# Linear attention and a GEGLU block on one core: block 1's halved units parted at column 320, one attention tile moved ahead of a transposing load, preps spread, one input load moved to another queue

## The chip, the cores and the metric

The kernel runs on one core of one Trainium2 chip. A core has TensorE (PE in the profile, its weight loads as PEld), VectorE (DVE), ScalarE (ACT), GpSimd (POOL) and SyncE (SP, which here only issues DMAs), and 16 DMA engines that all queues share. The metric is the device time of one execution in microseconds. Times are medians over several executions. A difference under about 0.3%, here 1 us, is about what a measurement of this kernel can't tell from no change.

## The reference

There are 8 batches of 8 heads, 576 positions, 64 features. The attention has no softmax; it is a product with cosine weights:

```python
theta = pi/2 * pos / S
phi(x) = concat([relu(x) * cos(theta), relu(x) * sin(theta)], axis=-1)   # 64 -> 128 features
kv  = einsum('bhsf,bhsd->bhfd', phi(k), v);   z = sum(phi(k), axis=2)
out = einsum('bhsf,bhfd->bhsd', phi(q), kv) / (einsum('bhsf,bhf->bhs', phi(q), z) + 1e-6)
```

The output, reshaped to 4608 tokens of 512, goes through a GEGLU block with 1536 hidden features: `(gelu(x @ w_gate) * (x @ w_val)) @ w_out`. Inputs and output are float32.

## The kernel before, in words

Everything on TensorE is in bf16. The 4608 tokens are cut into 9 blocks of 512 tokens, while a batch has 576, so blocks and batches drift apart by 64 tokens a batch: block 1 holds the last 64 tokens of batch 0 and the first 448 of batch 1, and block 2 holds the last 128 tokens of batch 1 and the first 384 of batch 2.

For a batch b these steps come in order:

- `prep` (lines 152 to 164) makes phi(q) and phi(k): for each of 9 position groups j, one instruction on VectorE for the cosine half (line 162) and one on ScalarE for the sine half (line 160), 128 x 256 each. This text writes them as q(b) and k(b) preps.
- `turn_q(b)` (line 191) turns phi(q) with two DMA transposes issued by SP (line 193) into `qT`. There is one `qT` buffer, so the next batch's transposes must wait until TensorE has read the last of the batch before.
- `kv_unit(b)` (line 235): 72 small matmuls (line 241) sum phi(k) and v, with a column of ones for z.
- `nm_unit(b, t)` (line 280), for each of five tiles t of 128 rows: 8 matmuls (line 282) for numerator and denominator, then on VectorE the added epsilon, the reciprocal and the product (lines 293 to 295) that gives the tile x(b, t).
- `turn_x(b, t)` (line 346) turns x(b, t) with DMA transposes by SP (line 349) into the columns of `xT` of one or two blocks; each block has its own `xT` buffer, three in turn.

For a block n, twelve units `gv_unit(n, jt)` (line 391) make the hidden features: 4 matmuls with gate weights into one PSUM bank, 4 with value weights into another (line 400), gelu on ScalarE (line 408, into `gel`) and the product on VectorE (line 409, into `hT`). Two pairs of banks alternate, so a unit's gate matmuls wait for the gelu of the unit two before it, and its value matmuls for that unit's product. `o_part` (line 427) does the output product (line 430), one third of a row tile between two units, and `store` (line 415) writes it out by SP.

All instructions stand in program order on each engine, and the order is written out by hand in the main loop (line 607 on). In the first blocks the first units are halved by columns (`heads`, line 616), since the later columns of `xT` come late: block 1 has six units halved at column 256 (`HALF`), run as six first halves and then six second halves. Columns 0 to 319 of block 1 need x(0,4), x(1,0) and x(1,1), which TensorE turns; columns 320 to 511 need x(1,2) and x(1,3), which the DMA transposes of line 349 bring. In the same stretch VectorE and ScalarE do the q(2) and k(2) preps, VectorE casts v(2) (line 179), and TensorE does the last tile of batch 1, `nm_unit(1, 4)`, after the sixth half. Its transposes `turn_x(1, 4)` are issued two steps later, followed by output stores.

The inputs come by two kinds of queue. GpSimd issues the weights and batches 1 and 2 and q(3) early on (lines 459 to 478); each input of a batch is loaded in two halves of 576 KB. SP issues batch 0, k(3), v(3), and then q, k and v of each later batch right after the turn of the batch before (`loads`, line 590, called in line 682). The staging buffers are two for each of q, k and v. The load of q(4) therefore goes into the buffer of q(2).

Of the kernel before, what the change touches and what calls it, by code (L numbers as in the profile page):

```python
# [16 lines left out]
def kernel(  # L17
# [13 lines left out]
    nc = tc.nc  # L31
# [8 lines left out]
    R = S // 64  # L40
    NB = B * S // 512
    NT = 5
    EPS = 1e-6
    BLK = 512
# [26 lines left out]
    def rows(t, b):  # L71
        return t[b].rearrange("(m i) (p j) d -> (i p) m (j d)", i=2, j=R)
# [4 lines left out]
    def load(eng, name, b, m0, m1, j0=0, j1=R):  # L77
        if (name, b) not in staged:
            staged[name, b] = inp.tile([128, NP, R * D], FP32, name=name + "f")
        eng.dma_start(  # L80
            out=staged[name, b][:, m0:m1, j0 * D:j1 * D],
            in_=rows(srcs[name], b)[:, m0:m1, j0 * D:j1 * D],
        )
# [51 lines left out]
    gate = consts.tile([128, 1], FP32)  # L135
# [16 lines left out]
    def prep(name, b, part, js, m0=0, m1=NP, eng=None):  # L152
        dst = phi_tile(name, b)
        src = staged[name, b]
        tab = (cos_t, sin_t)[part]
        for j in js:
            o = dst[:, m0:m1, j, part * D:(part + 1) * D]
            i = src[:, m0:m1, j * D:(j + 1) * D]
            if eng is nc.scalar:
                nc.scalar.activation(o, i, AF.Relu, scale=tab[:, j:j + 1])  # L160
            else:
                (eng or nc.vector).tensor_scalar(  # L162
                    o, i, 0.0, tab[:, j:j + 1], op0=ALU.max, op1=ALU.mult
                )
# [26 lines left out]
    def turn_q(b):  # L191
        for i in range(2):
            nc.sync.dma_start_transpose(
                out=qt_tile(b)[:, i].rearrange("f m (j p) -> f (m j) p", p=64),
                in_=phi["q", b][64 * i:64 * i + 64].rearrange("p m j f -> p (m j f)"),
            )
# [83 lines left out]
    def nm_unit(b, t, b0=6):  # L280
        for h in range(H):
            nc.tensor.matmul(  # L282
                bank(b0 + h // 4)[:, (h % 4) * (D + 1):(h % 4 + 1) * (D + 1)],
                lhsT=q_cols(b, t, h),
                rhs=kv_sb[b][:, h // 2, h % 2, :],
                start=True,
                stop=True,
            )
        nm = ps[:, b0:b0 + 2, 0:4 * (D + 1)].rearrange("p g (h d) -> p g h d", h=4)
        den = attn2.tile([128, 2, 4], FP32, name="den")  # L290
        rec = attn2.tile([128, 2, 4], FP32, name="rec")
        x = xsp.tile([128, 2, 4, D], BF16, name="x_sb")
        nc.vector.tensor_scalar_add(den, nm[:, :, :, D], EPS)
        nc.vector.reciprocal(rec, den)  # L294
        nc.vector.tensor_tensor(  # L295
            x,
            nm[:, :, :, 0:D],
            rec[:, :, :, None].to_broadcast([128, 2, 4, D]),
            op=ALU.mult,
        )  # L300
        xs[b, t] = x.rearrange("p g h d -> p (g h d)")
# [30 lines left out]
    def xT_block(blk):  # L332
        if blk not in xT:
            xT[blk] = xtp.tile([128, CT, BLK], BF16, name="xT")
        return xT[blk]
# [55 lines left out]
    def gv_unit(n, jt, c0=0, w=BLK):  # L391
        xt = xT[n]
        js = slice(jt * 128, (jt + 1) * 128)
        b0 = 2 * (turn[0] % 2)
        turn[0] += 1
        if n not in hT:
            hT[n] = ffn.tile([128, JT, BLK], BF16, name="hT")
        for g, wt in ((0, wg_sb), (1, wv_sb)):
            for ct in range(CT):
                nc.tensor.matmul(  # L400
                    bank(b0 + g)[:, 0:w],
                    lhsT=wt[:, ct, js],
                    rhs=xt[:, ct, c0:c0 + w],
                    start=(ct == 0),
                    stop=(ct == CT - 1),
                )
        gel = ffn.tile([128, BLK], FP32, name="gel")
        nc.scalar.activation(gel[:, 0:w], bank(b0)[:, 0:w], AF.Gelu)  # L408
        nc.vector.tensor_mul(  # L409
            hT[n][:, jt, c0:c0 + w], gel[:, 0:w], bank(b0 + 1)[:, 0:w]  # L410
        )
# [10 lines left out]
    def flush(n=4):  # L422
        for i, o_sb in stores[:n]:
            store((nc.sync, nc.sync), i, o_sb)
        del stores[:n]
# [19 lines left out]
    HALF = BLK // 2  # L445
# [144 lines left out]
    def loads(b, names=("q", "k", "v")):  # L590
        for name in names:
            for m in (0, 2):
                load(nc.sync, name, b, m, m + 2)
# [13 lines left out]
    for n in range(1, NB):  # L607
        b = n + 1
        t_kv, t_nm, t_q, t_k = {1: (7, 9, 12, 12), 2: (6, 7, 7, 9), 3: (2, 5, 6, 9)}.get(
            n, (1, 2, 4, 8)  # L610
        )
        for jt in range(JT):
            if n == 1 and jt >= t_nm:
                nm_unit(2, jt - t_nm, (6, 4, 6)[jt - t_nm])
                turn_x(2, jt - t_nm)
            heads = (0, 6, 4, 2)[n] if n < 4 else 0
            if jt >= heads:
                gv_unit(n, jt)
            else:
                for i in range(2):  # L620
                    half, unit = divmod(2 * jt + i, heads)
                    gv_unit(n, unit, half * HALF, HALF)
                    if n == 1 and jt < 2:
                        js = ((4,), (5,), (6,), (7, 8))[2 * jt + i]
                        prep("q", b, 1, js, eng=nc.scalar)
                        prep("q", b, 0, js)
                    if n == 1 and jt > 1:
                        j = 2 * jt - 4 + i
                        prep("k", b, 0, (j,))
                        prep("k", b, 1, (j,), eng=nc.scalar)  # L630
            if jt % 3 == 1 and n > 1:
                flush()
            if b < B:
                if n == 1 and jt == 1:
                    turn_q(b)
                if n == 1 and jt == 2:
                    nm_unit(1, NT - 1)
                if n == 1 and jt == 3:
                    turn_x(1, NT - 1)
                    flush()  # L640
                nms = [(b, jt - t_nm)] if n > 1 and 0 <= jt - t_nm < NT else []
                if n == 2 and jt < 2:
                    nms.append((n, 3 + jt))

                late = -(-(BLK - 64 * b) // 128)
                i = jt - t_nm - 1
                if n > 1 and 0 <= i < late:
                    turn_x(b, i)
                if n == 1 and jt == JT - 1:
                    loads(3, ("k", "v"))  # L650
                for bt in nms:
                    nm_unit(*bt)
                if jt == t_kv:
                    kv_unit(b)
                if n == 1 and jt == 6:
                    prep("k", b, 0, (R - 1,))
                    prep("k", b, 1, (R - 1,), eng=nc.scalar)
                if n == 2 and 3 <= jt < 6:
                    prep_third("k", b, jt - 3)
                i = 2 * (jt - 5) if n == 1 else jt - (4 if n == 2 else 0)  # L660
                if n == 1 and i == 0:
                    cast_v(b, 0, 4, dve_copy)
                if n in (2, 3) and 0 <= i < 2:
                    cast_v(b, 2 * i, 2 * i + 2, dve_copy)
                i = jt - 9
                if n > 2 and 0 <= i < 2 and b + 1 < B:
                    cast_v(b + 1, 2 * i, 2 * i + 2, dve_copy)
                if (n, jt) in q3:
                    cosines, sines_ = q3[n, jt]
                    prep("q", 3, 1, sines_, eng=nc.scalar)  # L670
                    prep("q", 3, 0, cosines)
                if n > 1 and b + 1 < B:
                    if 0 <= jt - t_q < 3:
                        prep_third("q", b + 1, jt - t_q)
                    if 0 <= jt - t_k < 3:
                        prep_third("k", b + 1, jt - t_k)
                for c, t in nms:
                    if t == NT - 1:
                        if c + 1 < B:
                            turn_q(c + 1)  # L680
                        if c + 2 < B:
                            loads(c + 2)
                        for i in range(-(-(BLK - 64 * c) // 128), NT):
                            turn_x(c, i)
            if n > 1:
                o_part(
                    4 * (n - 1) + jt // 3,
                    range(4 * (jt % 3), 4 * (jt % 3) + 4),
                    4,
                    act_copy,  # L690
                )
# [47 lines left out]
```

## Time and profile before

| what | value |
|---|---|
| median of 6 executions | 326.8 us (325.78 to 327.68) |
| the profiled execution | 325.78 us, of which the span is 323.6 us |
| granted TensorE clock | 0.999 |
| PE busy | 316.8 us (98% of the span) |
| DVE, ACT, POOL busy | 171.0, 159.0, 27.4 us (53%, 49%, 8%) |
| DMA | 53.83 MB, mean 166 GB/s |
| block 1's halved units | about 54.5 to 65.3 us after the span's start |
| block 1's full units, with kv_unit(2) | 65.3 to 77.9 us |
| first halved unit of block 2 | 77.85 us |

In the lines of the profile, "L400 PE MATMUL ps<-xT,wg_sb" means line 400, engine, operation, and what is written from what. A line of a timeline gives start and duration in microseconds, then the instruction and how many were merged, and in brackets the idle time of the engine before it with what ended it. A line of the chain gives start, duration and the work on the path that ended last. The page's row "DMA" holds the busy share of the DMA engines in tenths, in 40 equal slices of 8.09 us.

### The profile page before, as it was taken

How to read it: one execution, taken by the hardware profiler on the slowest of the kernel's cores; microseconds unless marked ns; L12 is line 12 of the kernel's file. 1: busy time of each engine (PE TensorE's matmuls, PEld its weight loads, DVE VectorE, ACT ScalarE, POOL GpSimd, SP SyncE). 2: the span in 40 equal slices, each digit the busy share in tenths (PEclk: the TensorE clock that was granted, in tenths of full speed). 3: DMA queues.
4: the chain of work that ended last, by engine and by line, in shares of the span. 5: the costliest groups of instructions: out<-in, count | busy, mean ns of one | idle time of the engine just before them, and what ended most of it. 6: DMA issues, size and time to landing. Idle time of an engine off the chain costs nothing.

```text
span 323.6 us, 6409 instructions
## 1 busy us (share of the span) xinstructions
PE 316.8 (98%) x2475; PEld 167.3 (52%) x2475; DVE 171.0 (53%) x411; ACT 159.0 (49%) x337; POOL 27.4 (8%) x45
## 2 busy tenths in 40 slices
PE   8899999999999999999999999999999999999995
PEld 3574556856754564545544554445544444444443
DVE  5854687859665952793686348544532222222211
ACT  7854757856466822673457336633222332222220
POOL 6675430000000000000000000000000000000000
PEclk9999999999999999999999999999999999999999
DMA  7999999963989689849956991563331111111124
GB/s 267 248 193 273 298 350 417 166 142 70 316 231 345 168 156 380 194 89 243 303 127 156 353 236 26 140 91 87 83 73 35 32 32 34 33 32 34 32 66 97
DMA packets 69966, 53.83 MB, mean 166 GB/s; under 512 B 46512, under 2 KB 55472, under 8 KB 69936
## 3 DMA queue, kind: packets, MB, share of 16 engines
q1 hardware_dynamic: 59840, 40.32, 48.8%
q0 software_dynamic: 9936, 12.98, 16.6%
q8 instruction: 19, 0.31, 0.4%
q10 hardware_dynamic: 160, 0.13, 0.1%
q14 instruction: 11, 0.09, 0.1%
HBM read 37.75 MB, written 9.44 MB: 146 GB/s over the span
## 4 chain that ended last, share of the span: by engine, by line
PE 93%; DMA 2%; DVE 2%; SPq 1%; issue 0%; DVEq 0%
PE ps L400 57%; PE ps L430 28%; PE ps L282 3%; PE ps L241 3%; DMA vf<-in_v_dram 2%; PE ps L372 1%; PE ps L204 1%; PE ps L700 1%; SPq L80 1%; DVE qp L162 0%; DVE x_sb L322 0%; PE ps L357 0%; DVE vx L179 0%; DVE x_sb L295 0%; DVE qT L485 0%
## 5 line engine op out<-in xcount | busy, mean ns | idle before, releaser
L409 DVE TENSOR_TENSOR hT<-gel,ps 128x512 bf16<-128x512 f32 (+1 forms) x118 | 74.7, 633 | 127.8 <-PE ps L400 124.9
L408 ACT ACTIVATE gel<-ps 128x512 f32<-128x512 f32 (+1 forms) x118 | 65.4, 554 | 109.1 <-PE ps L400 106.9
L400 PE MATMUL ps<-xT,wv_sb 128*128 128x512 bf16 (+1 forms) x472 | 110.9, 357 | 0.0
L400 PE MATMUL ps<-xT,wg_sb 128*128 128x512 bf16 (+1 forms) x472 | 110.9, 357 | 0.0
L430 PE MATMUL ps<-wo_sb,hT 128*128 128x512 bf16 x420 | 105.8, 379 | 0.0
L400 PEld LDWEIGHTS <-wv_sb 128*128 128x128 bf16 x472 | 46.2, 98 | 45.5
L400 PEld LDWEIGHTS <-wg_sb 128*128 128x128 bf16 x472 | 45.6, 98 | 44.9
L430 PEld LDWEIGHTS <-hT 128*128 128x128 bf16 x420 | 38.3, 98 | 39.4
L439 ACT COPY o_sb<-ps 128x512 f32<-128x512 f32 x34 | 19.9, 586 | 30.9 <-PE ps L430 30.7
L160 ACT ACTIVATE qp<-qf,sin_t 128x256 bf16<-128x256 f32 x72 | 31.7, 499 | 0.0
L160 ACT ACTIVATE kp<-kf,sin_t 128x256 bf16<-128x256 f32 (+1 forms) x73 | 30.5, 480 | 0.8 <-DMA kf<-in_k_dram 0.8
L295 DVE TENSOR_TENSOR x_sb<-ps,rec 128x512 bf16<-128x512 f32 x38 | 26.3, 691 | 1.3
L162 DVE TENSOR_SCALAR qp<-qf,cos_t 128x256 bf16<-128x256 f32 x71 | 21.8, 354 | 0.0
L162 DVE TENSOR_SCALAR kp<-kf,cos_t 128x256 bf16<-128x256 f32 x63 | 18.8, 350 | 0.0
L282 PEld LDWEIGHTS <-qT 128*128 128x128 bf16 x304 | 14.6, 98 | 7.7 <-ACT qT L485 0.3
L282 PE MATMUL ps<-kv_sb,qT 128*128 128x65 bf16 x304 | 16.0, 194 | 0.0
L179 DVE CAST vx<-vf 128x1152 bf16<-128x1152 f32 (+1 forms) x15 | 11.9, 802 | 1.0 <-DMA vf<-in_v_dram 1.0
L250 ACT CAST kv_sb<-ps 128x260 bf16<-128x260 f32 x14 | 4.6, 383 | 12.9 <-PE ps L241 12.9
L140 PE MATMUL ps<-dummy 128*128 128x512 bf16 x27 | 8.6, 467 | 1.5 <-POOL dummy L113 1.5
L241 PEld LDWEIGHTS <-kp 64*128 64x128 bf16 x504 | 8.5, 95 | 3.0 <-issue 3.0
L241 PE MATMUL ps<-vx,kp 64*128 64x65 bf16 x504 | 9.3, 191 | 0.0
L294 DVE RECIPROCAL rec<-den 128x8 f32<-128x8 f32 x38 | 7.7, 203 | 1.3
(60 smaller groups left out, 99.4 us busy)
## 6 DMA issues: line engine op xcount, KB each, us to landing
out_dram<-o_sb SPq DMA_DIRECT2D x70, 128.0 KB, 2.5
kf<-in_k_dram SPq DMA_DIRECT2D x12, 576.0 KB, 6.5
vf<-in_v_dram SPq DMA_DIRECT2D x12, 576.0 KB, 8.7
qf<-in_q_dram SPq DMA_DIRECT2D x8, 576.0 KB, 4.8
qf<-in_q_dram POOLq DMA_DIRECT2D x6, 576.0 KB, 12.1
kf<-in_k_dram POOLq DMA_DIRECT2D x4, 576.0 KB, 12.8
vf<-in_v_dram POOLq DMA_DIRECT2D x4, 576.0 KB, 12.9
wg_sb<-in_moe_w_gate_dram POOLq DMA_DIRECT2D x6, 256.0 KB, 6.6
```

What stands on the lines that cost most here:

```text
L140: nc.tensor.matmul(bank(to), lhsT=dummy[:, 0:128], rhs=dummy, start=True, stop=True)
L160: nc.scalar.activation(o, i, AF.Relu, scale=tab[:, j:j + 1])
L162: (eng or nc.vector).tensor_scalar(o, i, 0.0, tab[:, j:j + 1], op0=ALU.max, op1=ALU.mult)
L179: copy(vx_tiles[b % 2][:, m0:m1, j0:j1, 0:D], staged["v", b][:, m0:m1, j0 * D:j1 * D].rearrange("p m (j d) -> p m j d", d=D),)
L241: nc.tensor.matmul(bank(6 + i)[:, m * (D + 1):(m + 1) * (D + 1)], lhsT=kp[rr, m, j, :], rhs=vx[rr, m, j, :], start=(j == 0), stop=(j == R ...
L282: nc.tensor.matmul(bank(b0 + h // 4)[:, (h % 4) * (D + 1):(h % 4 + 1) * (D + 1)], lhsT=q_cols(b, t, h), rhs=kv_sb[b][:, h // 2, h % 2, :], ...
L295: nc.vector.tensor_tensor(x, nm[:, :, :, 0:D], rec[:, :, :, None].to_broadcast([128, 2, 4, D]), op=ALU.mult,)
L400: nc.tensor.matmul(bank(b0 + g)[:, 0:w], lhsT=wt[:, ct, js], rhs=xt[:, ct, c0:c0 + w], start=(ct == 0), stop=(ct == CT - 1),)
L408: nc.scalar.activation(gel[:, 0:w], bank(b0)[:, 0:w], AF.Gelu)
L409: nc.vector.tensor_mul(hT[n][:, jt, c0:c0 + w], gel[:, 0:w], bank(b0 + 1)[:, 0:w])
L430: nc.tensor.matmul(bank(to), lhsT=hT[n][:, jt, tt * 128:(tt + 1) * 128], rhs=wo_sb[:, jt, :], start=(jt == 0), stop=(jt == JT - 1),)
L439: copy(o_sb, bank(to))
```

## The change

Four things are done at once, all in the loop over blocks, at n = 1 but for the last line.

1. The six halved units of block 1 are parted at column 320 and not at 256: six first parts of 320 columns, then six second parts of 192.
2. `nm_unit(1, 4)` is moved up by two parts: after the fourth part and ahead of `turn_q(2)`, where it stood after the sixth part and behind `turn_q(2)`.
3. The k(2) preps, one for each of the last eight parts and one after the first full unit, are spread out: one after each of the last two 320-column parts, four after the six 192-column parts (two of these have none), and three after the first full unit.
4. q(4) is loaded by GpSimd. A copy of one column of block 2's `xT`, which `turn_x(1, 4)` writes, stands ahead of the two loads on GpSimd's queue, so that they wait for that transpose to land. SP loads only k(4) and v(4) after `turn_q(3)`.

```diff
             heads = (0, 6, 4, 2)[n] if n < 4 else 0
+            mid = 320 if n == 1 else HALF
             if jt >= heads:
                 gv_unit(n, jt)
             else:
                 for i in range(2):
                     half, unit = divmod(2 * jt + i, heads)
-                    gv_unit(n, unit, half * HALF, HALF)
+                    gv_unit(n, unit, *((mid, BLK - mid) if half else (0, mid)))
...
                     if n == 1 and jt > 1:
-                        j = 2 * jt - 4 + i
-                        prep("k", b, 0, (j,))
-                        prep("k", b, 1, (j,), eng=nc.scalar)
+                        js = ((0,), (1,), (2,), (), (3,), (), (4,), (5,))[2 * jt - 4 + i]
+                        prep("k", b, 0, js)
+                        prep("k", b, 1, js, eng=nc.scalar)
...
                 if n == 1 and jt == 1:
+                    nm_unit(1, NT - 1)
                     turn_q(b)
-                if n == 1 and jt == 2:
-                    nm_unit(1, NT - 1)
                 if n == 1 and jt == 3:
                     turn_x(1, NT - 1)
                     flush()
+
+                    nc.gpsimd.tensor_copy(gate, xT_block(2)[:, 0, 64:65])
+                    for m in (0, 2):
+                        load(nc.gpsimd, "q", 4, m, m + 2)
...
                 if n == 1 and jt == 6:
-                    prep("k", b, 0, (R - 1,))
-                    prep("k", b, 1, (R - 1,), eng=nc.scalar)
+                    prep("k", b, 0, (6, 7, 8))
+                    prep("k", b, 1, (6, 7, 8), eng=nc.scalar)
...
                         if c + 2 < B:
-                            loads(c + 2)
+                            loads(c + 2, ("k", "v") if c == 2 else ("q", "k", "v"))
```

## The prediction

> **What bounds the kernel now.** I read the page, TensorE's waits, the chain, the timelines around block 1, and last the DMA answers. First the page:
>
> ```profile
> PE 316.8 (98%) x2475; PEld 167.3 (52%) x2475; DVE 171.0 (53%) x411; ACT 159.0 (49%) x337; POOL 27.4 (8%) x45
> ```
>
> TensorE is busy 98% of the span. From 54 us on its wait list holds nothing but 2.5 us of issue time at six kv_units, which stay. An edit in block 1 can gain only what hides inside steps that look busy. The chain there, and its matmuls at the tail:
>
> ```profile
> 54.64 5.24 PE ps L400 x48
> 59.88 0.26 PE ps L282 x8
> 60.14 8.82 PE ps L400 x64
> ...
> 317.27 2.63 PE ps L700 x24
> ```
>
> The reader is to see back-to-back work: 5.24/48 = 109 ns a halved matmul. One gap shows when TensorE's timeline is compared at two nm_units:
>
> ```profile
> 59.72 0.42 PE L282 MATMUL ps<-kv_sb,qT 128*128 128x65 bf16 x8
> 60.11 0.60 PE L400 MATMUL ps<-xT,wg_sb 128*128 128x256 bf16 x4
> ...
> 71.90 0.42 PE L282 MATMUL ps<-kv_sb,qT 128*128 128x65 bf16 x8
> 72.16 1.02 PE L400 MATMUL ps<-xT,wg_sb 128*128 128x512 bf16 x4
> ```
>
> The next matmul starts 0.39 us after the first of them and 0.26 us after the second, so 0.13 us is lost at 60 us, where the second column halves begin. What they wait for shows in SP's timeline and the landing times of its transposes:
>
> ```profile
> 53.92 3.87 SPq L349 DMA_TRANSPOSE xT<-x_sb  x3
> 57.89 1.18 SPq L420 DMA_DIRECT2D out_dram<-o_sb  x2
> 60.22 7.39 SPq L193 DMA_TRANSPOSE qT<-qp  x2
> 67.71 1.20 SPq L349 DMA_TRANSPOSE xT<-x_sb  x1
> 68.95 3.85 SPq L420 DMA_DIRECT2D out_dram<-o_sb  x4
> 74.19 5.16 SPq L349 DMA_TRANSPOSE xT<-x_sb  x3
> ```
>
> Of the first three, those issued at 53.92 and 55.33 bring block 1's columns; asked one at a time they take 5.8 and 4.7 us, so they land at 59.7 and 60.0. The one at 74.19, with quiet queues, takes 2.5 us. The difference is GpSimd's load queue (49 to 59.5 us):
>
> ```profile
> q0 software_dynamic: 795, 3.21, 74.7%
> q1 hardware_dynamic: 1292, 0.56, 36.4%
> ```
>
> Its last load, half of q(3) issued at 47.40, takes 12.0 us and lands at 59.4; the transposes land just behind it.
>
> **The change part by part.**
>
> Parting at 320, TensorE's work. A 512-column matmul takes 216 ns (1.73/8), a 256 one 109, so 0.42 ns a column; that gives 136 ns for 320 and 82 for 192. The tail (L700) has 12 of each in 2.63 us, 219 ns a pair against 218 for two of 256. Over 48 pairs: +0.04 us. "TensorE: Matmul & The Clock Gate", section "LDWEIGHTS (loading the stationary operand)", of the Trainium skill speaks against this part: a load of 128 columns takes 128/1.2 = 107 ns, longer than a 192-column matmul. An estimate by that page, with each short matmul waiting for its load, would be 48 x (107 - 82) = +1.2 us. The L700 row, with a fresh load for each matmul, shows 82 ns paid and not 107, and line 372's 32 matmuls of 128 columns in 1.79 us (56 ns) say the same; I go by the rows.
>
> Parting at 320, the wait. Six first parts take 48 x 0.136 = 6.53 us; with the moved nm_unit (0.26) the second parts begin at 54.48 + 6.53 + 0.26 = 61.27 instead of 60.11. Their columns landed at 60.0, so the 0.13 us goes and 1.2 us of room appears.
>
> The moved nm_unit, on VectorE. Starts of successive instructions on VectorE give 0.34 us a 256 product (0.60 for 512), hence 0.40 for 320 and 0.27 for 192; a prep 0.26; den, rec and x 0.19 + 0.24 + 0.61 = 1.04. Starts of successive ones on ScalarE give gelu 0.28 (0.50 for 512), hence 0.33 and 0.23; a prep 0.40. From a group's end to VectorE's start takes 0.27 us (63.60 to 63.87). Walk: part 3 ends at 58.82, its product runs 59.09 to 59.49, two q preps to 60.02, the nm_unit's three to 61.06. Behind them is queued the product of part 4, ready at 60.44: it runs 61.06 to about 61.54. Part 6 wants that product's bank for its value matmuls at 61.27 + 0.33 = 61.60, with a release of about 0.1 (landing at 60.0, matmul at 60.11): 0.05 us late. Part 7 is as close, at 62.25 to 62.30. Before, the same three ran 60.59 to 61.71 behind a later part, with 0.25 us over. Bounds: nothing to 0.3 us; below nothing is excluded, since an earlier bank can't speed matmuls already back to back. I take 0.1, nearest the walk.
>
> The moved nm_unit, on SP. turn_q(2) now waits for the last q(2) prep on VectorE, 60.11, not for TensorE's reading of qT: still about 60.2, between 60.1 and 60.5. Its user at 71.90 has 2.8 us of cover (63.62 + 5.5 = 69.1), so zero.
>
> k(2) preps. The total stays; only the last three move later. ScalarE: gelu of the first full unit from 66.28, three preps 66.78 to 68.08, the next gelu at 68.01 or so: no wait beyond 0.1, and value matmuls cover that. VectorE: cast of v(2) to 67.28, product to 67.89, preps to 68.76. kv_unit(2) starts at 68.76 and wants groups 6, 7, 8 at 68.97 and later (72 in 1.27 us, so 35 ns a pair): cover 0.2 us. If it fails, 0 to 0.2 us; I take zero.
>
> q(4) by GpSimd. Its queue is idle after 48.1, so nothing stands behind the wait but the two loads. turn_x(1,4) lands at 67.71 + 2.3 = 70.0; copy 0.2 to 0.8, two issues of 0.7. SP saves two issues (92.99 to 94.04) ahead of k(4), v(4) and the transposes at 96.61, which took 9.7 us but are first needed by block 3 at 112.35: 1 us earlier there is worth zero. q(4) itself landed at 93.55 + 5.2 = 98.75, and ScalarE's first prep of it ran at 99.51: 0.75 us of room, now some 20. What can suffer is x(2,0), issued at 74.19, landing at 76.7, needed by block 2's first part at 77.85 - 0.1: 1.05 us of room. When q(4) lands is not shown; ends: a 576 KB half that SP issued alone at 79.45 took 3.9 us and two loads in a full queue landed 1.4 us apart (57.4 to 59.4 at the slowest, 2.0), so 75.7 to 76.3; or the 12.1 us of GpSimd's busy time, 82. I take the first, since the queues are nearly empty then: x(2,0) shares the engines for part of a microsecond, cost zero, and as ends 0 and the price of the collision below. "DMA: Bandwidth & Descriptors", section "SWDGE vs HWDGE vs iDMA", of the skill says that an engine takes turns between the two kinds of queue, so x(2,0) would be shared with and not parked behind q(4); the 5.8 us of the transpose at 53.92 show how dear sharing can be.
>
> Sum for the profiled execution: -0.13 + 0.04 + 0.1 = 0. But that execution, 325.78 us, is the fastest of the six; the median is 1.02 above it, and the change must be compared there. The wait at 60 us ends with a transpose behind a full load queue, so slower loading lands on TensorE one for one, and the change's 1.2 us of room takes it. The other open place is the start, where the chain has 7.9 us of DMA. No trace shows how the 1.02 us divides: between 0 and 1.02. I take half, 0.5. So 326.8 - 0.5 = 326.3.
>
> **The rivals.**
>
> All of the median's excess sits at waits that the change gives room: the one at 60 us, and q(4)'s landing 0.75 us ahead of its use. 326.8 - 1.02 = 325.8, and 325.7 with VectorE on time. For it: the room at 60 us is used up even in the fastest run, and a spread of 0.6% wants a loose place. Against: the initial loads are on the path too.
>
> q(4) collides with x(2,0) (the opposite side): were x(2,0) to take the 5.8 us of 53.92 instead of 2.5, it would land at 80.0, 2.3 us late, 326.8 + 2.3 = 329.1 less what is gained; near 328.3 for half of that. It decides from 3.5 us of transpose time on, that is, when q(4) holds the engines past about 76.4. For it: the ends above reach 76.3. Against: from 74.2 to 77.8 the DMA engines were only 30% busy.
>
> VectorE is later than walked: each 0.1 us at part 4's product costs 0.1 us; with an extra 0.5, and kv_unit(2) late by 0.2, 327.0.
>
> The change does nothing that shows: no gain at the wait, 326.8.
>
> **How the numbers follow.** Half the excess 0.40 (326.3, own range 325.8 to 326.8), all of it 0.30 (325.7), collision 0.15, late VectorE 0.10, nothing 0.05. The bound of 0.3%, about what a measurement here can tell from no change, lies at 325.8 and 327.8. The second case ends almost on it, so I count 0.7 of it beyond. Faster: 0.21 of that and 0.04 of the first, 0.25. Slower: 0.13 of the collision and 0.03 of late VectorE, 0.16. Same: 0.59. The range reaches from 325.3, the second case with a little noise of the median, to 327.9, the near part of the collision; about 0.18 is left out.
>
> **What would show it.** Right: after the moved nm_unit the next matmul follows in 0.26 us; the 192 parts begin near 61.3; the transposes of 53.92 land before that; q(4) issues near 70.5 and lands by 76.5; the matmul after block 1 starts near 77.8. Wrong: gaps of the value matmuls after 61.6 (VectorE), a gap ahead of block 2's first part (collision), 192-column matmuls over 82 ns, or a median that stays 1 us above the fastest run, which would put the excess at the start.

## The result and the profile after

The changed kernel is slower: a median of 327.75 us over 22 executions (326.51 to 330.28), against 326.39 us over 46 of the kernel before in the same sessions. The ratio is 1.0043, with a 95% interval of 1.0032 to 1.0055, so about 1.4 us. The forecast was 326.3 us in a range of 325.3 to 327.9; the median lies at the upper end of that range and on the side that was given the least chance, 0.16.

The profiled execution took 328.38 us, 0.6 above its own median, while that of the kernel before, 325.78, lay 0.6 below its median; so the two traces differ by 2.6 us and show the loss at more than its usual size. Row 1 of its page, the engines' busy time, share of the span and instructions:

```profile
PE 316.6 (97%) x2475; PEld 166.4 (51%) x2475; DVE 170.9 (52%) x411; ACT 159.1 (49%) x337; POOL 28.9 (9%) x48
```

TensorE is busy for the same time as before, 316.6 against 316.8 us, in a span 3.0 us longer. The time went into idling, not into work. TensorE's timeline after, at the moved nm_unit, at the turn from 320 to 192 columns, and at the end of block 1:

```profile
59.14 0.42 PE L282 MATMUL ps<-kv_sb,qT 128*128 128x65 bf16 x8
59.40 0.70 PE L400 MATMUL ps<-xT,wg_sb 128*128 128x320 bf16 x4
...
61.03 0.71 PE L400 MATMUL ps<-xT,wv_sb 128*128 128x320 bf16 x4
61.57 0.49 PE L400 MATMUL ps<-xT,wg_sb 128*128 128x192 bf16 x4
61.91 0.49 PE L400 MATMUL ps<-xT,wv_sb 128*128 128x192 bf16 x4
62.24 0.49 PE L400 MATMUL ps<-xT,wg_sb 128*128 128x192 bf16 x4
...
77.18 1.03 PE L400 MATMUL ps<-xT,wv_sb 128*128 128x512 bf16 x4
80.29 0.60 PE L400 MATMUL ps<-xT,wg_sb 128*128 128x256 bf16 x4 [2.08 <-issue]
```

Read the starts. After the moved nm_unit the next matmul follows in 0.26 us, so the 0.13 us at 60 us is gone. Four matmuls of 320 columns take 0.54 us and four of 192 take 0.33, that is 136 and 83 ns, with no gap where the widths change. Then block 2's first part starts at 80.29 us. The four value matmuls before it take 0.86 us, from 77.18 to 78.05, so TensorE loses 2.24 us there. The bracket names no releaser ("issue"); SP's queue, GpSimd's queue and the landing times do. SP after:

```profile
68.07 1.19 SPq L349 DMA_TRANSPOSE xT<-x_sb  x1
69.31 3.37 SPq L420 DMA_DIRECT2D out_dram<-o_sb  x4
74.38 5.16 SPq L349 DMA_TRANSPOSE xT<-x_sb  x3
```

GpSimd after:

```profile
70.42 0.17 POOL L642 CAST gate<-xT 128x1 f32<-128x1 bf16 x1 [22.12 <-DMA xT<-x_sb]
71.01 1.42 POOL L80 DMA_DIRECT2D qf<-in_q_dram  x2 [0.41 <-ACT kv_sb L250]
```

The DMA issues after, two windows, with the time from issue to landing in the last column: GpSimd's two loads (their median), and the transpose issued at 74.38:

```profile
qf<-in_q_dram POOLq DMA_DIRECT2D x2, 576.0 KB, 7.2
...
xT<-x_sb SPq DMA_TRANSPOSE x1, 5.8
```

x(2,0)'s transpose is issued near its old time (74.38 against 74.19), but takes 5.8 us where it took 2.5, and lands at 80.2. q(4)'s halves land at 77.8 and 79.4 in the trace. Block 2's first part starts 0.1 us after x(2,0) is there.

A second difference stands at the very end of the span. The last row of the chain is the last copy on VectorE; both kernels do the same stores behind it. Before, then after:

```profile
320.00 0.36 DVE o_sb L707
...
322.44 0.36 DVE o_sb L711
```

After, from its end, 322.80, to the end of the span, 326.6, it is 3.8 us. Before, it was 320.36 to 323.65 with one more digit, 3.3 us; counted from the last matmul's start in the traces, 4.52 against 4.00.

The spans add up: block 1 starts 0.32 us later, though both programs do the same work up to there (in the traces of all twelve kernels it starts between 54.5 and 55.7 us); the wait at 60 us goes, -0.13; block 2's first part, +2.24; the end, +0.52. The sum is 2.95 us, all of the difference of the spans.

The metric is the device time of an execution, though, and it doesn't hold all of the 0.52. The part of it that lies outside the span is 1.78 us by the mean of the changed kernel's executions (1.74 to 1.84), and 2.15 in 29 executions of the kernel before (2.08 to 2.21). So 0.36 of the 0.52 us stands against time saved outside the span, and about 0.15 us is lost at the end. In device time the two profiled executions differ by 2.60 us, 0.35 less than in their spans.

### The profile page after: what moved, and what is told of

It is laid out like the page before. It is cut to its first block, busy times and chain, and to the rows that moved or that the text cites. A ratio compares the mean times of both kernels' runs of the same rounds, so it can differ in the third digit from the quotient of the medians.

```text
span 326.6 us, 6417 instructions
## 1 busy us (share of the span) xinstructions
PE 316.6 (97%) x2475; PEld 166.4 (51%) x2475; DVE 170.9 (52%) x411; ACT 159.1 (49%) x337; POOL 28.9 (9%) x48
## 4 chain that ended last, share of the span: by engine, by line
PE 92%; DMA 4%; issue 1%; POOL 1%; DVE 0%; SPq 0%; ACT 0%; DVEq 0%
PE ps L400 56%; PE ps L430 28%; PE ps L282 3%; PE ps L241 3%; DMA vf<-in_v_dram 2%; DMA wv_sb<-in_moe_w_val_dram 2%; PE ps L704 1%; PE ps L372 1%; PE ps L204 1%; SPq L80 0%; PE ps L357 0%; ACT qp L160 0%; POOL wg_sb L94 0%; POOL gate L459 0%; DVE x_sb L295 0%
## 5 line engine op out<-in xcount | busy, mean ns | idle before, releaser
L409 DVE TENSOR_TENSOR hT<-gel,ps 128x512 bf16<-128x512 f32 (+3 forms) x118 | 74.7, 633 | 130.1 <-PE ps L400 127.4
L408 ACT ACTIVATE gel<-ps 128x512 f32<-128x512 f32 (+3 forms) x118 | 65.4, 554 | 111.1 <-PE ps L400 110.4
L400 PE MATMUL ps<-xT,wg_sb 128*128 128x512 bf16 (+3 forms) x472 | 110.9, 357 | 2.1 <-issue 2.1
L400 PE MATMUL ps<-xT,wv_sb 128*128 128x512 bf16 (+3 forms) x472 | 110.9, 357 | 0.0
```

The source lines that it names most:

```text
L400: nc.tensor.matmul(bank(b0 + g)[:, 0:w], lhsT=wt[:, ct, js], rhs=xt[:, ct, c0:c0 + w], start=(ct == 0), stop=(ct == CT - 1),)
L409: nc.vector.tensor_mul(hT[n][:, jt, c0:c0 + w], gel[:, 0:w], bank(b0 + 1)[:, 0:w])
```

## The experiments

Ten kernels were run, all against the kernel before on the same chip. Two questions had to be told apart: which of the four parts costs the time, and, once that was the load of q(4), whether its place, its size or its queue does it.

**Parts 1 to 3 without part 4.** The changed kernel less the lines of q(4):

```diff
-                    nc.gpsimd.tensor_copy(gate, xT_block(2)[:, 0, 64:65])
-                    for m in (0, 2):
-                        load(nc.gpsimd, "q", 4, m, m + 2)
...
-                            loads(c + 2, ("k", "v") if c == 2 else ("q", "k", "v"))
+                            loads(c + 2)
```

> The changed kernel without its fourth part: q(4) is loaded by SP behind q(3)'s turn, as before. Theory (q(4)'s early load stretches the transposes of x(2,0)): those land 2.5 us after their issue again, no gap ahead of block 2's first part, the 0.13 us at 60 us stays gone, and the time is that of the kernel before or up to 0.2 us less. If half of the median's 1.0 us over the fastest run sat at the wait at 60 us, as predicted, 0.5 us less than before. Rival (the narrow parts, the moved nm_unit or the late preps cost the time): at least 1 us more than before, with gaps of TensorE between 61 and 69 us.

Measured: a ratio of 0.9991 (0.9982 to 1.0), a median of 325.97 us against 326.58. The chain from 59 to 82 us in this run:

```profile
59.30 0.26 PE ps L282 x8
59.56 9.59 PE ps L400 x80
...
76.48 3.47 PE ps L400 x24
```

No gap ahead of block 2's first part, which lies inside the last row; x(2,0) lands 2.5 us after its issue. Parts 1 to 3 gain some 0.3 us by the ratio, 0.6 by the medians, though the interval reaches no change. They don't cost the time.

**Part 4 alone.** The kernel before, with part 4's lines added and nothing else.

> The kernel before with the fourth part alone: q(4) by GpSimd behind the landing of x(1,4)'s turn. Theory (collision): x(2,0)'s transposes take 5 to 6 us instead of 2.5, block 2's first part starts about 2 us late, and the time is 1.4 to 2.3 us over the kernel before, 0.13 us more than the changed kernel. Rival (parts 1 to 3 cost the time): within 0.3 us of the kernel before.

Measured: 1.0059 (1.0047 to 1.0071), about 1.9 us, median 328.4 us. Block 2's first part comes 1.68 us late, with x(2,0) at 5.2 us. The rival that puts the cost on parts 1 to 3 falls. TensorE's timeline in this run, at the old wait:

```profile
59.95 0.42 PE L282 MATMUL ps<-kv_sb,qT 128*128 128x65 bf16 x8
61.18 0.60 PE L400 MATMUL ps<-xT,wg_sb 128*128 128x256 bf16 x4 [0.81 <-DMA xT<-x_sb]
```

The next matmul follows nm_unit after 1.23 us instead of 0.26: here the wait at 60 us is 0.97 us, and the bracket now names the transpose. The work up to this point is the same as in the kernel before, whose profile showed 0.13. So this wait does vary from execution to execution.

**The same load later.** GpSimd's wait now stands behind the last turn of batch 2's first three tiles:

```diff
                 turn_x(2, jt - t_nm)
+                if jt == JT - 1:
+                    nc.gpsimd.tensor_copy(gate, xT_block(2)[:, 0, 448:449])
+                    for m in (0, 2):
+                        load(nc.gpsimd, "q", 4, m, m + 2)
```

> The changed kernel, with GpSimd's wait moved behind the landing of x(2,2)'s turn, so that q(4) is issued at about 81 us. Theory (collision): x(2,0) takes 2.5 us, no gap ahead of block 2's first part; q(4) now runs beside k(3), v(3) and q(3)'s turn, whose user comes 5 us after its landing in the kernel before, so a delay of some 3 us there is covered; time within 0.3 us of the run without part 4. Rival (loading by GpSimd costs by itself, wherever it is put): 1 us or more over the kernel before.

Measured: 0.9997 (0.9986 to 1.0009), by the ratios 0.2 us over the run without part 4, by the medians 0.7. SP's timeline:

```profile
75.11 5.15 SPq L349 DMA_TRANSPOSE xT<-x_sb  x3
80.37 1.03 SPq L80 DMA_DIRECT2D kf<-in_k_dram  x2
81.50 1.02 SPq L80 DMA_DIRECT2D vf<-in_v_dram  x2
85.53 12.16 SPq L193 DMA_TRANSPOSE qT<-qp  x2
```

x(2,0) takes 2.5 us again and there is no gap. The traffic now falls on q(3)'s turn, whose two issues take 12.2 us where they took 8.3 before; it lands at 99.2, and its user starts at 100.6, so 1.4 us of cover are left. The collision is there, but on a transpose that nobody waits for.

**The same load by SP.** At part 4's place, `load(nc.sync, ...)` and no copy by GpSimd:

> The changed kernel with q(4) at the same place in the program, but issued by SP behind the output stores at about 72.5 us and ahead of x(2,0)'s turn. If any 1.15 MB of traffic at that time stretches the transposes, x(2,0) takes 4 to 6 us and the time is 1 to 2.3 us over the kernel before. If it is GpSimd's queue that does it, x(2,0) takes 2.5 to 3.5 us, which its 1.05 us of room covers, and the time is that of the run without part 4.

Measured: 1.0029 (1.0014 to 1.0043). SP's timeline, and the landing time of the first of the three transposes:

```profile
73.66 1.07 SPq L80 DMA_DIRECT2D qf<-in_q_dram  x2
74.83 5.08 SPq L349 DMA_TRANSPOSE xT<-x_sb  x3
```

```profile
xT<-x_sb SPq DMA_TRANSPOSE x1, 5.2
```

q(4) lands at 78.0 and 79.5 in the trace, x(2,0) at 80.0, and block 2's first part is 1.69 us late. Such traffic does it from either queue; the kind of queue isn't the cause. How the transpose is held may still differ, since here it stands behind q(4) in one queue.

**Half of it.** The first half by GpSimd behind the wait, the second by SP ahead of k(4):

```diff
-                    for m in (0, 2):
-                        load(nc.gpsimd, "q", 4, m, m + 2)
+                    load(nc.gpsimd, "q", 4, 0, 2)
...
+                            if c == 2:
+                                load(nc.sync, "q", 4, 2, 4)
```

> The changed kernel with only the first half of q(4) issued by GpSimd behind the wait; SP loads the second half ahead of k(4) as before. If the collision is a matter of when the traffic ends, this half lands by 75.5 to 76.5 us, x(2,0) takes 2.5 to 3.5 us and its room covers that: no gap ahead of block 2's first part, and what is left over the run without part 4 is the 0.5 us at the program's end. If a transpose is parked by any traffic that is still going when it starts, whatever its size, x(2,0) lands after 78 and the gap is 0.3 to 1.5 us.

Measured: 0.9996 (0.9987 to 1.0005). The landing times of the half and of x(2,0):

```profile
qf<-in_q_dram POOLq DMA_DIRECT2D x1, 576.0 KB, 5.3
...
xT<-x_sb SPq DMA_TRANSPOSE x1, 2.5
```

The half, issued at 70.56, lands at 75.8, where x(2,0)'s packets start at about 75.4 to 75.5: the overlap is nearly nil, x(2,0) takes its 2.5 us and there is no gap. This is the edge. It also gives a price that the prediction lacked: one half, alone on GpSimd's queue and beside SP's last output stores, takes 5.3 us.

**No wait at all.** Only the copy is left out, so q(4) goes out beside q(2)'s turn:

> The changed kernel without GpSimd's wait: q(4)'s loads go out as soon as q(2)'s preps have left the buffer, at about 60.3 us, beside q(2)'s turn. In the runs so far a transpose that starts while a load is going lands 0.3 to 0.7 us after the load has. By that q(4), with 5.3 us for a half alone and 7 to 8.5 for both, lands at 67 to 69, q(2)'s turn at 70 to 72 instead of 69.6, against its user at 72.1; x(2,0), at 74.4, is clear of it and takes 2.5 us. So no gap ahead of block 2's first part, 0 to 0.5 us ahead of nm_unit(2,0), the 0.5 us at the program's end, and 0 to 0.3% over the kernel before. If part 4 is dear wherever its traffic meets a transpose, 1 us or more over the kernel before.

Measured: 1.0044 (1.0021 to 1.0067), about 1.4 us. It is the second case that came, 1 us or more, and not the 0 to 0.3% that was held likelier, though the interval reaches down into it. The issues of q(2)'s turn, then TensorE's timeline:

```profile
qT<-qp SPq DMA_TRANSPOSE x2, 9.3
```

```profile
72.96 0.19 PE L282 MATMUL ps<-kv_sb,qT 128*128 128x65 bf16 x1
74.24 0.40 PE L282 MATMUL ps<-kv_sb,qT 128*128 128x65 bf16 x7 [1.09 <-DMA qT<-qp]
```

q(2)'s two transposes take 9.3 us each by the median instead of 5.5, and nm_unit(2,0) waits 1.26 us in the midst of its eight matmuls, between the two halves of the turn. Its 2.8 us of cover didn't hold. x(2,0) is clear at 2.5 us. Moving the load doesn't remove the collision, it only picks the transpose that pays.

**Column 320 alone.** The kernel before, with `mid = 320` and nothing else changed:

> The kernel before with the first part alone: six units parted at column 320, the order of nm_unit(1,4) and of the preps as before. The runs with and without this part showed a wait at 60 us of 0.13 us (kernel before) and 0.97 us (part 4 alone), and none at 61 us where the parting is at 320. If that wait makes the gain of parts 1 to 3 (ratio 0.9991), this run has it whole: no gap at 61 us, 0.2 to 0.7 us less than the kernel before. If the moved nm_unit and the preps make it, this run is within 0.1 us of the kernel before.

Measured: 1.0006 (0.9994 to 1.0019), not the gain that was expected. The old wait is gone, but another has come. TensorE, then VectorE, in this run:

```profile
62.91 0.49 PE L400 MATMUL ps<-xT,wg_sb 128*128 128x192 bf16 x4
63.70 0.49 PE L400 MATMUL ps<-xT,wv_sb 128*128 128x192 bf16 x4 [0.30 <-DVE hT L409]
```

```profile
62.27 0.16 DVE L293 TENSOR_SCALAR den<-ps 128x8 f32<-128x8 f32 x1
62.46 0.20 DVE L294 RECIPROCAL rec<-den 128x8 f32<-128x8 f32 x1
62.70 0.69 DVE L295 TENSOR_TENSOR x_sb<-ps,rec 128x512 bf16<-128x512 f32 x1
63.31 0.34 DVE L409 TENSOR_TENSOR hT<-gel,ps 128x192 bf16<-128x192 f32 x1
```

With nm_unit(1,4) in its old place, its 1.04 us on VectorE come between the narrow parts and push the product behind them to 63.31; the value matmuls of 63.24 wait for it until 63.70, 0.47 us.

**Parts 2 and 3 alone.** The run without part 4, with the parting back at 256:

> The kernel before with parts 2 and 3 alone (nm_unit(1,4) ahead of q(2)'s turn, k(2)'s preps in their new places), units parted at column 256. If the wait at 60 us makes the gain of parts 1 to 3, it is there again, 0.1 to 1.0 us by where the transposes of x(1,3) land (59.9 to 61.0 in the runs so far), and the time is within 0.2 us of the kernel before. If parts 2 and 3 make the gain, 0.2 us or more less.

Measured: 1.0004 (0.9993 to 1.0016). The old wait is back, 0.89 us in this run, with the transpose of x(1,3) landing 5.4 us after its issue, at 61.7:

```profile
61.88 0.60 PE L400 MATMUL ps<-xT,wg_sb 128*128 128x256 bf16 x4 [0.72 <-DMA xT<-x_sb]
```

So neither part 1 nor parts 2 and 3 show a gain alone: in each trace one wait is left, and with all three, in the run without part 4, there is neither. The times agree with that but don't show it, since the three intervals overlap.

**Three copies on GpSimd, no load.** The run without part 4, with three copies of one column at part 4's place:

> The run without part 4, with three copies of one column by GpSimd at part 4's place (the first waits for x(1,4)'s turn as in part 4), but q(4) still loaded by SP. All three kernels with part 4's instructions end 4.5 us after the last matmul's start, the others 4.0. If it is more instructions on GpSimd, or later ones, that lengthens the end, this run has 4.5 too and is 0.5 us over the run without part 4. If it is GpSimd's late loads, 4.0 and no difference.

Measured: 0.9994 (0.9983 to 1.0006), a ratio that can't tell 0.4 us. The end of the span can, in the one trace of each kernel. The expectations count it from the start of the last matmul: 4.40 us here, 4.00 in the kernel before and without part 4, 4.50 to 4.56 in the four kernels with GpSimd's wait and load, and 4.66 with the load but no wait. The device time outside the span goes the other way: 1.78 to 1.80 us by the means of the kernels with a longer end, this one among them, and 2.14 to 2.16 of the others. So of the longer end some 0.04 us here and up to 0.3 with the load but no wait is device time. The ratios of this run and of the half, 0.9994 and 0.9996 against 0.9991, fit such a size better than 0.5 us, but don't exclude it.

**Three copies on GpSimd, early.** The same copies at 10 us:

> The run without part 4, with three tiny copies added to GpSimd ahead of the first weight load at about 10 us, none later. If the longer end comes from the number of GpSimd's instructions, the program ends 4.4 to 4.5 us after the last matmul's start. If it comes from GpSimd working late in the program, 4.0.

Measured in one execution: 326.25 us, 1.75 of it outside the span. The end takes 4.55 us from the last matmul's start. The chain's last row in this run, in a span of 324.5 us:

```profile
320.27 0.36 DVE o_sb L709
```

From 320.63 to the end it is 3.9 us, as in the changed kernel, though GpSimd does nothing late. More instructions on GpSimd lengthen the end of the span; when they run doesn't matter.

## Why the prediction was wrong

**The step that failed is q(4)'s landing.** The prediction took 75.7 to 76.3 us for it, from the half that SP issued at 79.45 (3.9 us) and a second 1.4 to 2.0 us behind, "since the queues are nearly empty then", and so costed the collision with x(2,0) at zero. The loads landed at 77.8 and 79.4. One half alone on GpSimd's queue takes 5.3 us, not 3.9, and the half at 79.45 wasn't alone either: k(3)'s second half, issued at 80.03, landed at 85.6, 2.3 us behind it. The two halves of q(4) ran beside the tail of the output stores and then beside the transposes, 7.2 us by the median. The prediction had named 76.4 us as the point from which the collision decides; both landings are past it. The Trainium skill's page "DMA: Bandwidth & Descriptors", section "Anatomy of one DMA — SWDGE (gpsimd) path", would have given 2.0 us and bytes over 436 GB/s, an estimate of 3.4 us for a half of 589,824 bytes; the 5.3 us measured decide.

**The rival had the right collision, place and price.** It put the transpose at 5.8 us under a load and the loss at 2.3 us; 5.8 us and 2.24 us came in the profiled execution, 5.2 us and 1.7 in two other runs. That the 5.8 agrees to the digit is in part luck: the profiled execution is 0.6 us above the median, and 327.75 lies below the rival's 329.1 less a gain of 0.3 to 0.6. What was wrong is its chance, 0.15, and the argument against it: that the DMA engines were 30% busy between 74.2 and 77.8 us said how free the window was before, not when a load put into it would leave. In the three kernels where q(4) meets x(2,0), the transpose lands 0.5 to 0.8 us after the load (80.2 after 79.4, 80.5 after 79.8, 80.0 after 79.5). That is no rule for every transpose: without the wait q(2)'s first one landed 0.2 us after q(4), and with the late load q(3)'s first one 2.8 us after it.

The prediction took from the skill's section "SWDGE vs HWDGE vs iDMA", on turns taken between the two kinds of queue, that x(2,0) would be shared with and not parked. The changed kernel's trace shows both. From 74.3 to 75.5 us GpSimd's queue moved 100 packets and SP's queue none, while an output store that SP had issued at 71.22, ahead of x(2,0), was still under way; it took 8.4 us, where the same store took 3.7 before. GpSimd's queue in that window, and the store's issue:

```profile
q0 software_dynamic: 100, 0.41, 95.5%
...
out_dram<-o_sb SPq DMA_DIRECT2D x1, 128.0 KB, 8.4
```

From 76.4 to 79.0 us both queues moved, SP's 589 packets and GpSimd's 38. So beside the load a plain store came late too, and not the transpose alone. The store isn't what x(2,0) waited for: with part 4 alone it had landed at 77.9, and x(2,0) still came at 80.5. What sets the landing of the transpose beyond that, the runs don't show.

**A term was missing, a small one.** Nothing in the sum stood for the program's end: 0.50 to 0.52 us of the span in the kernels with all of part 4's lines, of which about 0.15 us is device time. It was taken that GpSimd is idle after 48 us and so nothing stands behind. The two runs with copies show that it is the instructions themselves. Why, they don't show, nor why the time outside the span gets shorter. In the traces the pause of 0.4 us falls between GpSimd's own last instructions, one or two places earlier or later as more or fewer were added, which would fit a fixed place in its program; that is only argued.

**The base was off.** The prediction took 326.8 us, the median of six executions, and an excess of 1.02 over the fastest. The median of 46 is 326.39, 0.6 above the profiled execution, so its 326.3 would have been hardly a gain.

**Right, as far as the runs show.** The wait at 60 us: the prediction read 0.13 us from two starts and said that the slower executions lose more there, taking 0.5. Runs with the old parting showed 0.13, 0.97 and 0.89, and parts 1 to 3 gain 0.3 by the ratio and 0.6 by the medians, with an interval from nothing to 0.6; the half was near, and the rival that gave it all of the 1.02 was too high. The 1.2 us of room wasn't always enough: with half of q(4), where x(1,3) landed at 61.4, 0.12 us was still lost. VectorE's walk: with block 1 starting 0.32 later, the product of part 4 was due at 61.38. VectorE's timeline after:

```profile
60.77 0.69 DVE L295 TENSOR_TENSOR x_sb<-ps,rec 128x512 bf16<-128x512 f32 x1
61.38 0.48 DVE L409 TENSOR_TENSOR hT<-gel,ps 128x320 bf16<-128x320 f32 x1
```

It ended at 61.86 and the value matmuls started at 61.91, on time: cost 0 where 0.1 was taken. The 192-column matmuls paid 83 ns, as the tail's row said, and not the 107 that the skill's page "TensorE: Matmul & The Clock Gate", section "LDWEIGHTS (loading the stationary operand)", would let one fear. The k(2) preps cost nothing.

The whole by the runs: parts 1 to 3 -0.3 us; part 4 +1.9 us, of which about 0.15 at the end and the rest the collision, 1.68 in its trace. Their sum, 1.6, stands against 1.4 measured. Of all versions tried, parts 1 to 3 without part 4 have the lowest ratio, 0.9991 of the kernel before, which isn't clear of no change.

## What to carry to other kernels

In these runs a gap in the DMA row was room only for a transfer that had left it again when the next transpose's packets started; so time the landing of a load of the same size on the same queue, not of a quicker neighbour. Look at every transpose under the load and ask who waits for it: the same 1.15 MB cost nothing over q(3)'s turn, 1.3 us over q(2)'s and 1.7 to 2.2 over x(2,0)'s. A parting that gives a transfer room can take it from the engine that works behind it (0.47 us on VectorE with column 320 alone), so look whether the work of that engine has to move along with it. And before a longer span is called a loss, compare the time outside it.

## What the runs showed that was not expected

Two or three more instructions on GpSimd, even early ones of under 0.2 us without any load, lengthened the end of the span by 0.4 to 0.66 us, in all seven kernels that had them, the changed one among them; the four others run, and the kernel before, ended alike to 0.01 us. In the same seven the device time outside the span is 0.36 to 0.41 us shorter, so that little of it is lost.

The loads were slower on GpSimd's queue than on SP's: half of q(4) alone landed after 5.3 us, and of the two halves the first took 6.8 and the second 7.7, where SP's two, issued 2.6 us later at the same place of the program, took 4.3 and 5.2. Whether the other half, the stores or the transpose slows them on GpSimd's queue, no run tells apart.
